# Moving a chunk's word preparation behind the activation's copy on ScalarE, in the first block of an attention, FFN and routed-experts kernel

## The chip, the cores and the metric

The program runs on one core of a Trainium2 chip. Its time is device microseconds (us) of one execution; the kernel before takes 1396.14 us (median of 3 runs, 1395.46 to 1397.46). Five engines work beside each other, each through its own instructions in order: PE (TensorE, matmuls), DVE (VectorE), ACT (ScalarE), POOL (GpSimd) and SP (SyncE, here only an issuer of DMAs). They wait for one another by semaphores.

## The reference, cut to what matters

```python
# 1. attention over 8-fold pooled keys and values, 8 batches x 8 heads, 576 tokens, head size 64
k_p = k.reshape(B, H, 72, 8, D).mean(axis=3); v_p = (the same of v)
attn = softmax(q @ k_p.T / sqrt(D))          # 72 scores a token and head
x = (attn @ v_p) as rows of 512              # 4608 tokens
# 2. a dense FFN, 512 -> 2048 -> 512
h = x @ w_in
g = where(h >= 1, h, where(h <= -1, 0, (h + 1) ** 2 / 4))
x = g @ w_out
# 3. routing to one of 8 experts (512 -> 1024 -> 512, relu), weighted by the gate's probability
out[tokens of e] = gate * (relu(x @ w1[e]) @ w2[e])
```

The dense FFN's weights come in a 64-bit format: `w_in` and `w_out` are read as pairs of 32-bit words, and the kernel makes float32 numbers of them itself.

## The kernel before, in words

The 4608 tokens are 36 tiles of 128 and go through the dense FFN in ten blocks of 3, 4, ..., 4, 3 and 2 tiles. A block runs over 16 chunks `m` of the hidden width. For each chunk, `f1(j, m)` (lines 614 to 643) makes the hidden values of 128 columns for the block's tokens, in one of two PSUM banks (`ps[m % 2]`, the names ps_72 and ps_73), and `f2(j, m)` multiplies them with the chunk's rows of `w_out`. Every product is taken in three matmuls, high by high, high by low and low by high, so each factor is split into a high part (a copy that rounds) and a low part (the difference). `f1` runs two chunks ahead of `f2`.

The activation of a chunk is a relay: DVE clips (L626), ACT squares (L627), DVE takes the larger of that and the hidden value, in the PSUM bank (L631), ACT copies it as the high part (L632), DVE subtracts for the low part (L266 with FG as its output). The next chunk but one overwrites the bank, so its `f1` comes behind that L266. L631 and L632 stand in a function `larger`, L266 in `lower`; both are not issued at once but put on a list `later`, which `flush()` works off. `larger` puts `lower` on the list when it runs, so that comes one flush later.

Between the products of a chunk stand two slots, `slot(j, 2 * m)` behind `f1` and `slot(j, 2 * m + 1)` behind `f2`. A slot runs some units of the attention for the next block's tiles (transpose of the queries L384 and its copy L386; scores L327 with maximum L334 and difference L336; exp L341; sum L394; turning L414 and L416; a way through DRAM, L417 and L423; the product with the values L443 and its copies L449 and L450) and ends with a flush.

In the first block the weights aren't there yet. A `tick` stands at the head of each of the slots 0 to 23. It converts: for the weight chunk at hand, `convert_a` (two ACT instructions, L545 and L549) scales the high words and prepares their sign; `convert_b` puts two DVE instructions (L557 and L560, integer shifts that join the words, through PSUM) on a list `pend`, which `mix()` works off, a call at a time, at certain places of the units and in `f1`, and which the next tick's `mix(4)` empties; two ticks later `convert_c` splits the result (ACT L571, high; POOL L266 with W or WO, low). An even slot's tick splits a chunk of `w_out` (WO), an odd slot's a chunk of `w_in` (W). The next words from DRAM are loaded into the buffer that the tick before has read (L530, L533, on SP).

Because `larger` lies on the list when an even slot begins and the flush stands at the slot's end, ACT's order in an even slot is: square, split (L571), L545, L549, the copies of the units, then L632. The first chunks are converted in a head section, the last ones of it (ticks 4 to 7) between the first two `f1`.

Of the kernel before, what the change touches and what calls it, by code (L numbers as in the profile page):

```python
# [24 lines left out]
def attention_ffn_routed_experts_kernel(  # L25
# [244 lines left out]
    def mix(n=1):  # L270
        for _ in range(min(n, len(pend))):
            pend.popleft()()
# [3 lines left out]
    def flush():  # L276
        for _ in range(len(later)):
            later.popleft()()
# [284 lines left out]
    def convert_ab(i):  # L563
        convert_a(i)
        convert_b(i)

    def convert_c(i):
        m, o = order[i]
        dst, _ = cvt_dst(i)
        hi, lo = (WO[:, m % 4, 0], WO[:, m % 4, 1]) if o else (wi4(m, 0), wi4(m, 1))  # L570
        nc.scalar.activation(out=hi, in_=dst, func=ACTF.Copy)  # L571
        low_part(lo, dst, hi)
        if o:
            nc.sync.dma_start(out=r32(wo_d[m]), in_=r32(WO[:, m % 4]))
# [15 lines left out]
    def more_raw(i):  # L590
        if i < len(order) and order[i]:
            load_raw(*order[i], i % NRB)

    def tick(late=False):

        n = ticks[0]
        mix(4)
        if n > 0:
            more_raw(n - 1 + NRB)
        if 0 <= n - 2 < len(order) and n != 3:  # L600
            convert_c(n - 2)
        if n < len(order):
            if late:
                later.append(lambda: convert_ab(n))
            else:
                convert_ab(n)
        ticks[0] += 1
# [5 lines left out]
    def f1(j, m):  # L613
        g = j * KF + m
        n = blocks[j][1] * 128
        o = ps[m % 2][:, 0:n]
        for c in range(KD):
            xh, xl = XT[:, j % 2, 0, c, 0:n], XT[:, j % 2, 1, c, 0:n]
            nc.tensor.matmul(o, wi(m, 0, c), xh, start=(c == 0), stop=False)  # L619
            nc.tensor.matmul(o, wi(m, 0, c), xl, start=False, stop=False)  # L620
            nc.tensor.matmul(o, wi(m, 1, c), xh, start=False, stop=(c == KD - 1))  # L621
        r = (JK if j == 0 and m % 2 else FR)[:, 0:n]
        gh, gl = FG[:, g % (AHEAD + 1), 0, 0:n], FG[:, g % (AHEAD + 1), 1, 0:n]


        nc.vector.tensor_scalar(r, o, -1.0, 1.0, op0=ALU.max, op1=ALU.min)  # L626
        nc.scalar.activation(out=r, in_=r, func=ACTF.Square, scale=0.5, bias=half)  # L627
        mix()

        def larger():  # L630
            nc.vector.tensor_tensor(out=o, in0=r, in1=o, op=ALU.max)  # L631
            nc.scalar.activation(out=gh, in_=o, func=ACTF.Copy)  # L632
            if KF <= g + 1 < len(steps):
                load_out(g + 1)
            later.append(lower)

        def lower():
            low_part(gl, o, gh, nc.vector)
        later.append(larger)
# [163 lines left out]
    def pick_first():  # L803
        V = nc.vector
        cnt = CB[:, 0]
        mx, mn = MX4[:, 0], MN4[:, 0]
        g = G1[:, 0]
        V.tensor_reduce(out=mx, in_=cnt, axis=AX.X, op=ALU.max)
        V.tensor_scalar(g, cnt, mx, None, op0=ALU.is_equal)
        V.scalar_tensor_tensor(out=g, in0=g, scalar=-16.0, in1=iota4[:, 0], op0=ALU.mult,  # L810
                               op1=ALU.add)
        V.tensor_reduce(out=mn, in_=g, axis=AX.X, op=ALU.min)
        V.tensor_scalar(FST, g, mn, None, op0=ALU.is_equal)
        V.tensor_scalar(FSI, mn, 16.0, None, op0=ALU.add)
        V.tensor_copy(FSR, FSI)

        V.tensor_scalar(POS0, FSI, -float(CAP), -float(EARLY * 128), op0=ALU.mult, op1=ALU.add)
        for t in range(LN):
            V.tensor_scalar(IDF[:, t:t + 1], pcol, float((blocks[-1][0] + t) * 128 - NT), None,
                            op0=ALU.add)  # L820
# [4 lines left out]
    def fetch_first(dst, t0, n):  # L825
        r = nc.values_load(FSR[0:1, 0:1], engines=[SP], min_val=0, max_val=NE - 1)
        nc.sync.dma_start(out=dst, in_=tiles_of[:, bass.ds(r, 1), t0:t0 + n].rearrange(
            "p o r -> p (o r)"))
# [5 lines left out]
    def load_first(i):  # L834
        if not first:
            first.append(nc.values_load(FSR[0:1, 0:1], engines=[ACT], min_val=0, max_val=NE - 1))
        src = (w1, w2)[i // 4][bass.ds(first[0], 1)].rearrange("o (c p) f -> p (o c) f", p=128)

        if i < 4:
            nc.scalar.dma_start(out=ST1[:, i:i + 1], in_=src[:, i:i + 1])  # L840
        else:
            nc.scalar.dma_start(out=ST2[:, 2 * i - 8:2 * i - 6], in_=src[:, 2 * i - 8:2 * i - 6])
# [129 lines left out]
    def q_gather(qn, i):  # L972
        gather(XG[i], q_ids(qn, i), qn == 0)

    def q_tx(qn, i):
        xb, cs = (NB + qn) % 2, slice(i * 128, (i + 1) * 128)
        u_tx(XG[i], XT[:, xb, 0, :, cs], XT[:, xb, 1, :, cs], q_gate(qn, i))
# [104 lines left out]
    def cvt1(c):  # L1082
        nc.scalar.activation(out=e1(0)[:, c], in_=ST1[:, c], func=ACTF.Copy)
        low_part(e1(1)[:, c], ST1[:, c], e1(0)[:, c])

    def cvt2(hf, i):
        cs = slice(4 * hf + 2 * i, 4 * hf + 2 * i + 2)
        nc.scalar.activation(out=e2(0)[:, cs], in_=ST2[:, cs], func=ACTF.Copy)
        nc.vector.tensor_tensor(out=e2(1)[:, cs], in0=ST2[:, cs], in1=r32(e2(0)[:, cs]),
                                op=ALU.subtract)  # L1090
# [41 lines left out]
    with tc.manual_schedule():  # L1132
# [9 lines left out]
        def run_units(n):  # L1142
            for _ in range(n):
                units.popleft()[1]()
            if qloads:
                qloads.popleft()()
# [79 lines left out]
        def slot(j, s):  # L1226

            want = min(state["units"], -(-(s + 1) * state["units"] // (22 if j == NB - 2 else 29 - 2 * AHEAD + 2)))
            wide[0] = False
            if j == 0:  # L1230
                for _ in range(min(1, PER[s // 2]) if s % 2 == 0 else PER[s // 2] - 1):
                    tick()
            run_units(want - state["done"])
            state["done"] = max(want, state["done"])
            flush()
            if j == 0 and kv:
                kv.popleft()()
            for _ in range(2 if j >= NB - 2 else 0 if wide[0] else 1 + s % 2):
                if todo:
                    todo.popleft()()  # L1240
            if j == PICK + 2 and s == 0:
                pick_first()
            for i in range(8):
                if 32 * (j - NB + 2) + s == LF[i]:
                    load_first(i)
            if j == NB - 2:

                if s == 1:
                    fetch_first(IDA, 0, EARLY)
                if s == 9:  # L1250
                    for i in range(EARLY):
                        q_gather(0, i)
            if j == NB - 1:
                if s == 3:
                    nc.gpsimd.iota(IO, pattern=[[1, 128]], base=0, channel_multiplier=0,
                                   allow_small_or_imprecise_dtypes=True)
                if s == 17:
                    fetch_first(IDQ, EARLY, 4 * NQ)
                if s == 27:
                    nc.vector.tensor_copy(IDMF, IDQ)  # L1260
                if s in CV1:
                    cvt1(CV1.index(s))
                if s in QT0:
                    q_tx(0, QT0.index(s))
                if s in (25, 27):
                    cvt2(0, (s - 25) // 2)

        for m in range(AHEAD):
            f1(0, m)
            flush()  # L1270
            while ticks[0] < CAHEAD + 2 + m:
                tick()
                flush()
        for g, (j, m) in enumerate(steps):
            if m == 0:
# [22 lines left out]
            else:  # L1298
                f1e(0, g + AHEAD - len(steps))
            slot(j, 2 * m)  # L1300
            f2(j, m)
            if (j, m) == (0, KF - 2):
# [4 lines left out]
                nc.gpsimd.iota(pr, pattern=[[0, NE * NTILE]], base=NT, channel_multiplier=1)  # L1307
                nc.sync.dma_start(out=perm_t, in_=pr)
            slot(j, 2 * m + 1)
        evict_y(NB - 1)  # L1310
        st, scatters = route_steps(NB - 1, bank)
# [186 lines left out]
```

## Time and profile before

| | |
|---|---|
| median of 3 runs | 1396.14 us |
| the profiled execution | 1394.67 us |
| its span in the trace | 1393.0 us |
| PE busy | 1353.9 us (97%) |
| DVE, ACT, POOL busy | 762.4, 433.3, 355.5 us |

PE's busy share is in tenths 7 7 8 8 in the first four of 40 slices of 34.8 us and 9 in nearly all behind them. The first block's `f1` of chunk 0 starts at 30 us, that of chunk 2 at 36 us and the second block's first `f1` at 138.58 us; this is the stretch that the change touches. Times in the rows are us from the span's start; a duration in a timeline is that of one instruction with its latency, and the next of the same engine can start before it ends.

### The profile page before, as it was taken

What the parts mean: (1) busy time and instruction counts of PE and PEld (TensorE: products, weight loads), DVE (VectorE), ACT (ScalarE), POOL (GpSimd) and SP (SyncE); (2) the same over time, 40 slices, a digit from 0 to 9 for tenths busy, and PEclk for the clock granted to TensorE, in tenths of its full rate; (3) what the DMA queues carried; (4) which work ended last, traced back from release to release, by engine and by line L of the source; (5) the groups of instructions that cost most, each with busy time, mean ns of one, the idle gap of its engine ahead of it and who ended that gap; (6) DMA issues with size and microseconds to landing.
All of it is one profiled execution on the core that took longest, in us unless ns stands there. A gap on an engine that the chain in (4) does not pass through costs nothing. (4 is left out here: it accounts for less than half of the span.)

```text
span 1393.0 us, 22129 instructions
## 1 busy us (share of the span) xinstructions
PE 1353.9 (97%) x8114; PEld 1111.7 (80%) x8114; DVE 762.4 (55%) x1539; ACT 433.3 (31%) x730; POOL 355.5 (26%) x517
## 2 busy tenths in 40 slices
PE   7788999999999999999999999999999999999998
PEld 6666778888778788788788788889878888888886
DVE  5698566656666675566666556455532323323426
ACT  5667232222222222222222233343121111111335
POOL 4475636004304203313310011021231211111211
PEclk9899999999999999999999999999999999999999
DMA  9986656546637555555453344572543223331235
GB/s 235 287 274 221 186 144 193 144 123 176 179 116 197 149 161 155 159 166 150 148 158 111 111 142 146 187 264 79 182 137 107 92 72 109 104 107 59 86 125 188
DMA packets 170702, 213.48 MB, mean 153 GB/s; under 512 B 83431, under 2 KB 114439, under 8 KB 170568
## 3 DMA queue, kind: packets, MB, share of 16 engines
q1 hardware_dynamic: 135992, 102.29, 25.7%
q10 hardware_dynamic: 26784, 88.16, 18.9%
q0 software_dynamic: 7792, 21.35, 4.7%
q8 instruction: 71, 1.16, 0.4%
q14 instruction: 63, 0.52, 0.1%
HBM read 188.30 MB, written 47.03 MB: 169 GB/s over the span
## 5 line engine op out<-in xcount | busy, mean ns | idle before, releaser
L619 PE MATMUL ps<-XT,W 128*128 128x512 f32 (+2 forms) x640 | 243.3, 380 | 5.3 <-ACT W L571 2.4
L621 PE MATMUL ps<-XT,W 128*128 128x512 f32 (+2 forms) x640 | 237.6, 371 | 2.2 <-POOL W L266 2.2
L620 PE MATMUL ps<-XT,W 128*128 128x512 f32 (+2 forms) x640 | 237.6, 371 | 0.5 <-DVE XT L450 0.5
L647 PE MATMUL ps<-WO,FG 128*128 128x512 f32 x576 | 231.2, 401 | 1.0 <-ACT Y L656 1.0
L648 PE MATMUL ps<-WO,FG 128*128 128x512 f32 x576 | 225.9, 392 | 0.0
L649 PE MATMUL ps<-WO,FG 128*128 128x512 f32 x576 | 225.3, 391 | 0.0
L627 ACT ACTIVATE FX<-FX,half 128x512 f32<-128x512 f32 (+2 forms) x152 | 104.0, 684 | 379.7 <-DVE FX L626 357.9
L626 DVE TENSOR_SCALAR FX<-ps 128x512 f32<-128x512 f32 (+2 forms) x152 | 96.9, 638 | 122.0 <-PE ps L621 121.5
L619 PEld LDWEIGHTS ps<-XT,W 128*128 128x128 f32 x640 | 121.3, 190 | 30.4 <-ACT W L571 3.6
L745 POOL DMA_INDIRECT perm_d<-idt,POSI x36 | 35.2, 978 | 424.3 <-DVE SM L731 357.5
L621 PEld LDWEIGHTS ps<-XT,W 128*128 128x128 f32 x640 | 121.3, 190 | 21.4 <-POOL W L266 3.4
L1019 DVE SCALAR_TENSOR_TENSOR FG<-ps,FG 128x512 fp32r<-128x512 f32 (+1 forms) x64 | 43.2, 674 | 173.3 <-ACT FG L1018 173.3
L631 DVE TENSOR_TENSOR ps<-FX,ps 128x512 f32<-128x512 f32 (+2 forms) x152 | 97.6, 642 | 73.5 <-ACT FX L627 73.5
L620 PEld LDWEIGHTS ps<-XT,W 128*128 128x128 f32 x640 | 121.4, 190 | 18.4 <-DVE XT L450 1.1
L647 PEld LDWEIGHTS ps<-WO,FG 128*128 128x128 f32 x576 | 108.4, 188 | 25.7 <-issue 2.8
L632 ACT ACTIVATE FG<-ps 128x512 fp32r<-128x512 f32 (+2 forms) x160 | 88.8, 555 | 125.4 <-DVE ps L631 116.8
L649 PEld LDWEIGHTS ps<-WO,FG 128*128 128x128 f32 x576 | 108.6, 188 | 23.5
L266 DVE TENSOR_TENSOR FG<-ps,FG 128x512 fp32r<-128x512 f32 (+2 forms) x160 | 100.8, 630 | 44.6 <-ACT FG L632 43.1
L648 PEld LDWEIGHTS ps<-WO,FG 128*128 128x128 f32 x576 | 108.6, 188 | 19.8
L1018 ACT ACTIVATE FG<-ps 128x512 fp32r<-128x512 f32 (+1 forms) x64 | 37.4, 584 | 244.1 <-PE ps L1015 230.5
L254 POOL TENSOR_TENSOR AT<-AT 72x256 f32<-72x256 f32 x104 | 79.2, 762 | 128.9 <-DMA AT<-in_v_dram 67.7
L1013 PE MATMUL ps<-XT,W 128*128 128x512 f32 (+1 forms) x256 | 99.0, 387 | 2.9 <-ACT XT L997 2.5
(235 smaller groups left out, 2157.8 us busy)
## 6 DMA issues: line engine op xcount, KB each, us to landing
WO<-wo_d ACTq DMA_DIRECT2D x144, 512.0 KB
AT<-in_moe_w_dram SPq DMA_DIRECT2D x30, 1024.0 KB
p_d<-AT SPq DMA_DIRECT2D x29, 384.0 KB
AT<-in_v_dram SPq DMA_DIRECT2D x59, 144.0 KB
wo_d<-WO SPq DMA_DIRECT2D x16, 512.0 KB
AT<-in_k_dram SPq DMA_DIRECT2D x56, 144.0 KB
PT<-p_d SPq DMA_DIRECT2D x58, 128.0 KB
yrow_d<-Y ACTq DMA_DIRECT2D x7, 1032.0 KB
```

The lines of the kernel that those rows point to most:

```text
L266: eng.tensor_tensor(out=lo, in0=x, in1=r32(hi), op=ALU.subtract)
L619: nc.tensor.matmul(o, wi(m, 0, c), xh, start=(c == 0), stop=False)
L620: nc.tensor.matmul(o, wi(m, 0, c), xl, start=False, stop=False)
L621: nc.tensor.matmul(o, wi(m, 1, c), xh, start=False, stop=(c == KD - 1))
L626: nc.vector.tensor_scalar(r, o, -1.0, 1.0, op0=ALU.max, op1=ALU.min)
L627: nc.scalar.activation(out=r, in_=r, func=ACTF.Square, scale=0.5, bias=half)
L631: nc.vector.tensor_tensor(out=o, in0=r, in1=o, op=ALU.max)
L632: nc.scalar.activation(out=gh, in_=o, func=ACTF.Copy)
L647: nc.tensor.matmul(o, gh, WO[:, g % 4, 0], start=(m == 0), stop=False)
L648: nc.tensor.matmul(o, gh, WO[:, g % 4, 1], start=False, stop=False)
L649: nc.tensor.matmul(o, gl, WO[:, g % 4, 0], start=False, stop=(m == KF - 1))
L1013: nc.tensor.matmul(o, e1(0)[:, c, ms], xh, start=(c == 0), stop=False)
```

## The change

In the first block's slots, and in the short loop that runs ticks 4 to 7, `tick` is called with `late=True`. This does what the head section has done already: `convert_a` and `convert_b` of the tick are put on the list `later` instead of being issued at once. In a slot the list then holds `larger` (or `lower`), `convert_a` with `convert_b`, and what the units add; so L545 and L549 come behind the units' copies and behind L632, and `pend` gets L557 and L560 only at the slot's end. The splits (`convert_c`) and the loads stay where they were. No instruction is added or taken away; PE's, POOL's and SP's orders are the same.

```diff
@@ slot(j, s)
             wide[0] = False
             if j == 0:
                 for _ in range(min(1, PER[s // 2]) if s % 2 == 0 else PER[s // 2] - 1):
-                    tick()
+                    tick(True)
             run_units(want - state["done"])
             state["done"] = max(want, state["done"])
             flush()
@@ before the main loop
             f1(0, m)
             flush()
             while ticks[0] < CAHEAD + 2 + m:
-                tick()
+                tick(True)
                 flush()
```

On ACT, two even slots of the first block, those of chunk 10 and, behind the "...", of chunk 11 (FX and AT hold the clipped values of even and odd chunks, FG the activation, Y, WG and AT also raw words; ps_78 and ps_79 are the units' banks):

```order
 L627 ACTIVATE FX<-FX,half 128x384
 L571 ACTIVATE WO<-FX 128x512
+L632 ACTIVATE FG<-ps_72 128x384
 L545 ACTIVATE FX<-Y 128x512
 L549 ACTIVATE WG<-Y 128x512
-L632 ACTIVATE FG<-ps_72 128x384
 L341 ACTIVATE AT<-AT 128x8x72
...
+L386 ACTIVATE AT<-ps_78 128x512
+L632 ACTIVATE FG<-ps_73 128x384
 L545 ACTIVATE FX<-AT 128x512
 L549 ACTIVATE WG<-AT 128x512
-L386 ACTIVATE AT<-ps_78 128x512
```

L632 has moved ahead of the pair L545, L549, and so has the unit's copy L386; all twelve even slots read so.

On DVE, the slot of chunk 10, where the unit of the scores stands (ps_77 is the bank through which L557 hands its result to L560):

```order
 L336 TENSOR_TENSOR AT<-ps_78,smx_124 128x4x72
 L334 TENSOR_REDUCE smx_124<-ps_79 128x4
+L336 TENSOR_TENSOR AT<-ps_79,smx_124 128x4x72
+L631 TENSOR_TENSOR ps_72<-FX,ps_72 128x384
 L557 SCALAR_TENSOR_TENSOR ps_77<-Y,WG 128x512
-L336 TENSOR_TENSOR AT<-ps_79,smx_124 128x4x72
-L631 TENSOR_TENSOR ps_72<-FX,ps_72 128x384
 L560 SCALAR_TENSOR_TENSOR FX<-FX,ps_77 128x512
 L266 TENSOR_TENSOR FG<-ps_72,FG 128x384
```

L557 has moved from ahead of L631 to behind it; this happens at chunks 7, 10 and 13. At two earlier places an odd slot's L557 moves from ahead of the second L336 to behind L266 and the next L626. In all other steps DVE's order is unchanged, and there L557 stood right behind L631 before too:

```order
L631 TENSOR_TENSOR ps_72<-FX,ps_72 128x384
L557 SCALAR_TENSOR_TENSOR ps_77<-AT,WG 128x512
L560 SCALAR_TENSOR_TENSOR FX<-FX,ps_77 128x512
L266 TENSOR_TENSOR FG<-ps_72,FG 128x384
L626 TENSOR_SCALAR AT<-ps_73 128x384
```

Nothing moved here (the step of chunk 8, the same in both kernels).

## Rows read from the trace of the kernel before

**Rows 1.** Stretches of 20 us: busy us (instructions) by engine, granted clock, DMA.

```profile
100.00:120.00 20.00, 15.78 (x117) 12.85 (x116) 18.75 (x32) 14.39 (x27) 9.21 (x7) 1.00 0.89 304
...
160.00:180.00 20.00, 20.00 (x134) 16.00 (x133) 9.72 (x16) 5.65 (x11) 10.15 (x19) 1.00 0.70 172
```

**Rows 2.** PE's waits, 36 to 160 us: total us, times, longest.

```profile
PE ps L443 <- DMA PT<-p_d: 5.1, 3, 2.5
PE ps L327 <- ACT AT L386: 3.9, 1, 3.9
```

**Rows 3.** Timeline of ACT, chunk 10: start, duration, instruction, [idle before <-releaser].

```profile
111.11 0.49 ACT L632 ACTIVATE FG<-ps 128x384 fp32r<-128x384 f32 x1 [2.79 <-DVE ps L631]
111.50 0.68 ACT L341 ACTIVATE AT<-AT 128x576 f32<-128x576 f32 x1
...
112.59 0.66 ACT L545 ACTIVATE FX<-Y 128x512 f32<-128x512 f32 x1
113.14 0.78 ACT L549 ACTIVATE WG<-Y 128x512 f16<-128x512 f32 x1
113.78 0.60 ACT L627 ACTIVATE AT<-AT,half 128x384 f32<-128x384 f32 x1
```

**Rows 4.** Timeline of DVE, chunks 10 to 13.

```profile
109.50 0.69 DVE L557 SCALAR_TENSOR_TENSOR ps<-Y,WG 128x512 int32<-128x512 int32 x1
110.09 0.45 DVE L336 TENSOR_TENSOR AT<-ps,smx 128x288 f32<-128x288 f32 x1
110.46 0.56 DVE L631 TENSOR_TENSOR ps<-FX,ps 128x384 f32<-128x384 f32 x1
110.92 0.68 DVE L560 SCALAR_TENSOR_TENSOR FX<-FX,ps 128x512 int32<-128x512 int32 x1
...
113.96 0.70 DVE L557 SCALAR_TENSOR_TENSOR ps<-Y,WG 128x512 int32<-128x512 int32 x1 [0.33 <-ACT WG L549]
...
115.37 0.56 DVE L631 TENSOR_TENSOR ps<-AT,ps 128x384 f32<-128x384 f32 x1
116.18 1.27 DVE L557 SCALAR_TENSOR_TENSOR ps<-AT,WG 128x512 int32<-128x512 int32 x1 [0.26 <-ACT WG L549]
...
121.98 0.69 DVE L450 SCALAR_TENSOR_TENSOR XT<-ps,XT 128x512 fp32r<-128x512 f32 x1 [1.48 <-ACT XT L449]
122.59 0.55 DVE L631 TENSOR_TENSOR ps<-FX,ps 128x384 f32<-128x384 f32 x1
123.05 0.69 DVE L557 SCALAR_TENSOR_TENSOR ps<-WG 128x512 int32<-128x512 int32 x1
...
130.93 0.56 DVE L266 TENSOR_TENSOR FG<-ps,FG 128x384 fp32r<-128x384 f32 x1
```

**Rows 5.** Timeline of PE: two matmuls of chunk 9, the first of chunk 15.

```profile
92.86 0.34 PE L620 MATMUL ps<-XT,W 128*128 128x384 f32 x1
...
94.64 0.52 PE L620 MATMUL ps<-XT,W 128*128 128x384 f32 x1
...
132.04 0.44 PE L619 MATMUL ps<-XT,W 128*128 128x384 f32 x1 [0.44 <-ACT W L571]
```

**Rows 6.** Timeline of DVE, the clip of chunk 3.

```profile
55.72 0.56 DVE L626 TENSOR_SCALAR AT<-ps 128x384 f32<-128x384 f32 x1 [4.62 <-PE ps L621]
```

**Rows 7.** DVE's groups, 28 to 145 us: count, busy us, mean ns, idle before.

```profile
L560 DVE SCALAR_TENSOR_TENSOR FX<-FX,ps 128x512 int32<-128x512 int32 x30 | 20.6, 686 | 1.6
L557 DVE SCALAR_TENSOR_TENSOR ps<-WG 128x512 int32<-128x512 int32 x15 | 15.5, 1032 | 1.7 <-ACT WG L549 1.6
L557 DVE SCALAR_TENSOR_TENSOR ps<-Y,WG 128x512 int32<-128x512 int32 x10 | 8.2, 818 | 1.0 <-ACT WG L549 1.0
...
L557 DVE SCALAR_TENSOR_TENSOR ps<-AT,WG 128x512 int32<-128x512 int32 x5 | 4.1, 820 | 2.5 <-ACT WG L549 2.5
```

**Rows 8.** Timeline of DVE, the longest L557.

```profile
98.58 3.17 DVE L557 SCALAR_TENSOR_TENSOR ps<-WG 128x512 int32<-128x512 int32 x1 [0.18 <-ACT WG L549]
```

**Rows 9.** Timeline of POOL beside it.

```profile
99.90 1.29 POOL L266 TENSOR_TENSOR WO<-FX,WO 128x512 fp32r<-128x512 f32 x1
```

## The prediction, before the result was known

> **What bounds the kernel now.** I read the busy shares by stretch first, then PE's waits in the first block, then the timelines of ACT and DVE side by side. Over the whole span PE is the bound. In the first block it is not: from 100 to 120 us PE is busy 15.78 of 20 us and DVE 18.75, while from 160 to 180 us, with the conversion over, PE is busy all of its 20 us and DVE 9.72 [rows 1]. So between about 65 and 135 us the relay of the activation and the conversion, run by DVE and ACT in turns, sets the pace and PE follows. What PE itself names as releaser there is small and mixed: 5.1 us for the transposed probabilities from DRAM, 3.9 us once for ACT's copy of the transposed queries [rows 2]. Whatever is lost or won in this block stays to the end, because behind it PE has no idle time to give back.
>
> **What the change moves.** No instruction comes or goes. In the loop for ticks 4 to 7 the list is flushed right behind the tick, and the order of every engine stays as it was: nothing. In the twelve even slots L545 and L549 go behind the units' copies and L632. Two things follow.
>
> What it gives: L386, L449 and L632 no longer stand behind a pair that takes 1.19 us of ACT (L545 starts at 112.59, the instruction behind L549 at 113.78) [rows 3].
>
> What it takes: L632 cannot start before DVE's L631, so now L545 and L549 cannot either, and DVE's next instruction behind L631 is L557, which needs L549. Before, ACT did this pair while DVE was still on its way to L631. Now DVE stands still while ACT does three instructions. The price from rows: L631 starts at 110.46 and L632 at 111.11, 0.65; L632 to the next ACT instruction 0.39; L545 to L549 0.55; L549 at 113.14 to DVE's L557 at 113.96, 0.82 [rows 3, 4]. From L631's start to L557's start that is 2.41 us, where DVE alone needs 0.46 (122.59 to 123.05) [rows 4]. DVE works in order, so everything behind L557 waits too: L560, L266 (for which PE's next `f1` but one waits, since it overwrites the bank), the clip L626 of the next chunk and the units. No operation here is new, but a wait is; its bounds are 0 (DVE would have stood idle anyway, as the 4.62 us before the clip of chunk 3 [rows 6]) and 1.95 us a chunk. I work with rows of three kinds of steps, which repeat every three chunks:
>
> - Chunk 10 (scores unit; L557 now behind L631): L631 comes 0.59 sooner, at 109.87, L557 at 109.87 + 2.41 = 112.28, L560 after its 0.69 at 112.97 instead of 110.92: 2.05 later.
> - Chunk 11: L557 followed L631 by 0.81 (115.37 to 116.18), now by 2.41; the 0.33 wait at 113.96 falls away, since DVE comes later and finds the signs there: 2.41 - 0.81 - 0.33 = 1.27 later.
> - Chunk 12: 2.41 instead of 0.46, but DVE had waited 1.48 for L449, which comes 1.19 sooner: 2.41 - 0.46 - 1.19 = 0.76 later [rows 4].
>
> Three chunks together: 4.08 us. DVE is busy 94% there [rows 1], so I see nothing that would swallow it.
>
> The sum, chunk by chunk. Chunks 2 and 3: L386 comes 1.19 sooner and PE's 3.9 us wait shrinks, but L557 of that slot is late and stands ahead of the scores' maximum on DVE; DVE then idles for PE (4.62 us [rows 6]). Between -1.2 and +1.9; I take 0. Chunks 4 to 6: DVE begins with idle time in hand, half of a full turn, 2.0. Chunks 7 to 9 and 10 to 12: two full turns, 8.2. Chunk 13: a step like chunk 10's, 2.05, less the slack of PE's `f1` of chunk 15, which starts at 132.04 and could have at 130.93 + 0.56 = 131.49 [rows 4, 5]: 1.5. Behind it no pair is left to move. Together 11.7.
>
> One term is open to both sides: how long L557 takes. Its thirty instances are busy 15.5 + 8.2 + 4.1 = 27.8 us, at L560's mean of 0.686 they would be 20.6: 7.2 us too long [rows 7], the worst 3.17 us, and that one ends 0.56 us after a POOL subtraction of 1.29 us that had begun at 99.90 [rows 8, 9]. L560 has one operand in PSUM, L557 both in SBUF. In the changed kernel the even slots' L557 starts some 2 us later against ACT's split of WO and so against POOL's subtraction behind it; it may miss it, or meet the pooling of the values. Bounds: all 7.2 goes, or all stays. I take half, 3.5, since the even slots hold half of the L557.
>
> The Trainium skill ("SBUF — State Buffer", section "Who interferes with whom") says that a DVE instruction with two SBUF inputs and a GpSimd instruction that reads SBUF exclude each other for a whole instruction, the later one standing still. The trace agrees as far as the rows above go: the long instances are all of L557, up to 3.17 us beside a POOL row. By that rule, if the late L557 missed POOL every time, the sum would be 11.7 - 7.2 = 4.5; by the rows' totals alone, unchanged, 11.7.
>
> Forecast: 11.7 - 3.5 = 8.2 us longer. The profiled execution's 1394.67 becomes 1402.9; the median lies 1.47 above it, so 1404.3 us.
>
> **The rivals.**
>
> 1. The new stall lies in idle time of DVE and only the gain remains. Place: the copies L386 and L449. Price: 1.19 us at the 3.9 us wait for L386 and at each of the three tiles' L449, 4 x 1.19 = 4.8 us shorter, 1391.3 us. It decides if DVE's idle time ahead of the clips is above 1.95 us in most chunks. For it: the 4.62 us at chunk 3 [rows 6]. Against: 1.25 us of idle time in 20 us, over three chunks [rows 1]. Chance 0.08.
>
> 2. A cover: PE waits for the transposed probabilities anyway, 5.1 us [rows 2], and works on in the meantime delayed but not idle; with all of L557's excess gone too, 11.7 - 5.1 - 7.2 = -0.6, 1395.5 us, no change. Against: the transfer starts from DVE's turning of the probabilities, which queues behind the same L557 and moves with it. Chance 0.11.
>
> 3. The clock. PE's matmuls of chunk 9 take 0.52 instead of 0.34 us behind waits of PE [rows 5]: 0.18 x 12 = 2.2 us for an `f1`. Two more such spells on the path: 8.2 + 4.3 = 12.5, 1408.6 us. For it: PE idles more in every chunk. Against: from 100 to 120 us PE idles 4.2 of 20 us and the granted clock is 1.00 [rows 1], and a slower `f1` ends long before DVE comes to its clip. Chance 0.15. The Trainium skill ("TensorE: Matmul & The Clock Gate", section "HAM oscillation — how this bites in real kernels") tells of loops whose repeated waits throw the array back to half rate each time; the row of 0.52 us agrees that it happens here, the stretch at 1.00 that it need not.
>
> That the change does something else than it says is excluded by the order of the instructions.
>
> **How the numbers follow.** Forecast 0.66, rivals 0.08, 0.11 and 0.15. The forecast's own ends are 4.5 (L557's excess gone) and 11.7 (all stays): 1400.6 to 1407.8. The range goes on to the slow clock with none of the excess gone, 11.7 + 4.3 = 16.0 at the worst, of which I take most, and below to 1399, between the forecast's lower end and the cover: 1399.0 to 1411.5. About 0.2% (2.8 us) is what a measurement tells from no change. Slower by more: forecast and clock, 0.81. Within: 0.11. Faster: 0.08.
>
> **What would show it right or wrong.** Right: DVE's idle time ahead of L557, put down to ACT's L549, rises from the 5.1 us of the groups [rows 7] to about 20 us, in pieces of 1.5 to 2 us, one to a chunk from 2 to 13; L632 follows L631 by 0.65 in each; the second block's first `f1` starts some 8 us later than at 138.58, and all behind it is shifted by the same. L557's busy total falls by some 3 us. The wait of 3.9 us for L386 shrinks by about 1.2. Wrong: if the stalls are there but the second block starts within 1 us of before, DVE had slack that I didn't see (rivals 1 and 2); if DVE stalls little, ACT's pair did not become part of the relay; if the shift is over 12 us with the granted clock well under 0.9 between 80 and 140 us, it is the clock.

## The result, and the profile after

The changed kernel takes 1404.45 us (median of 4 runs, 1403.74 to 1406.29) against 1396.57 us of the kernel before (4 runs beside it, 1395.46 to 1397.46). The ratio is 1.0066, 95% interval 1.0053 to 1.0078: slower by 9.2 us, 7.4 to 10.9 (here and below the differences in us are taken from such ratios; the two medians as they stand differ by 7.9). The forecast was 8.2 us longer. The span of the profiled execution grew from 1393.0 to 1403.0 us.

The stretches of 20 us of the changed kernel, in the columns of [rows 1]:

```profile
100.00:120.00 20.00, 15.93 (x123) 12.99 (x124) 14.21 (x27) 13.36 (x24) 7.63 (x6) 0.91 0.80 264
...
160.00:180.00 20.00, 20.00 (x133) 15.98 (x132) 11.59 (x21) 7.17 (x12) 11.29 (x22) 1.00 0.70 175
```

DVE was busy 18.75 us of the first stretch and is now busy 14.21: it stands still, though it sets the pace (the changed kernel is some 5 us behind by then, so the stretches don't hold quite the same work). Behind the block PE is again busy all the time, so nothing is given back.

Where DVE waits in the first block, before (28 to 145 us) and after (28 to 153 us); total us, times, longest:

```profile
DVE XT L450 <- ACT XT L449: 5.2, 5, 1.7
DVE ps L557 <- ACT WG L549: 5.1, 13, 1.1
DVE AT L626 <- PE ps L621: 4.6, 1, 4.6
DVE FX L626 <- PE ps L621: 4.1, 2, 2.7
```

```profile
DVE ps L557 <- ACT WG L549: 23.4, 15, 1.8
DVE AT L626 <- PE ps L621: 5.1, 1, 5.1
DVE XT L450 <- ACT XT L449: 4.2, 5, 1.8
DVE FX L626 <- PE ps L621: 1.7, 2, 1.3
```

One line has grown, by 18.3 us, and its longest is the stall of the forecast. The timelines of ACT and DVE at chunk 10, to be held against [rows 3, 4]:

```profile
115.42 0.49 ACT L632 ACTIVATE FG<-ps 128x384 fp32r<-128x384 f32 x1 [3.43 <-DVE ps L631]
115.80 0.65 ACT L545 ACTIVATE FX<-Y 128x512 f32<-128x512 f32 x1
116.35 0.77 ACT L549 ACTIVATE WG<-Y 128x512 f16<-128x512 f32 x1
```

```profile
114.77 0.55 DVE L631 TENSOR_TENSOR ps<-FX,ps 128x384 f32<-128x384 f32 x1
117.15 0.70 DVE L557 SCALAR_TENSOR_TENSOR ps<-Y,WG 128x512 int32<-128x512 int32 x1 [1.83 <-ACT WG L549]
...
119.86 0.51 DVE L626 TENSOR_SCALAR AT<-ps 128x384 f32<-128x384 f32 x1
...
124.79 0.70 DVE L557 SCALAR_TENSOR_TENSOR ps<-AT,WG 128x512 int32<-128x512 int32 x1 [1.80 <-ACT WG L549]
...
126.60 0.55 DVE L626 TENSOR_SCALAR FX<-ps 128x384 f32<-128x384 f32 x1
...
128.83 0.69 DVE L450 SCALAR_TENSOR_TENSOR XT<-ps,XT 128x512 fp32r<-128x512 f32 x1 [0.29 <-ACT XT L449]
129.44 0.55 DVE L631 TENSOR_TENSOR ps<-FX,ps 128x384 f32<-128x384 f32 x1
131.80 0.70 DVE L557 SCALAR_TENSOR_TENSOR ps<-WG 128x512 int32<-128x512 int32 x1 [1.80 <-ACT WG L549]
```

The relay reads off: L631 at 114.77, L632 at 115.42, L545, L549, L557 at 117.15, 2.38 us from first to last, with ACT idle 3.43 us ahead of it and DVE idle 1.83 us within it. There are twelve such stalls of 1.77 to 1.83 us, one for each chunk from 2 to 13. PE's waits, 36 to 170 us, beside [rows 2]:

```profile
PE ps L619 <- DVE FG L266: 12.1, 7, 2.4
PE ps L384 <- DVE AT L336: 5.2, 4, 2.4
PE ps L443 <- DMA PT<-p_d: 4.7, 3, 1.8
PE ps L327 <- ACT AT L386: 2.8, 1, 2.8
PE ps L327 <- ACT AT L288: 1.8, 1, 1.8
...
```

The wait for L386 is 1.1 us shorter, as the change meant it; the same scores then wait 1.8 us for L288, the copy of the transposed pooled keys, which ACT does behind L632 and so now behind the pair; I had not seen that. What has come is above all the first line: PE waits for the bank that L266 reads, and L266 stands behind L557 on DVE. The second block's first `f1`, at 138.58 us before, now reads (the first of its matmuls)

```profile
149.36 0.40 PE L619 MATMUL ps<-XT,W 128*128 128x512 f32 x1
```

All of DVE's first block lies 0.41 us later from its beginning (the first clip at 32.83 instead of 32.42 us), so the block itself is 10.37 us longer in this trace; below, "shift" is always this measure, with the run's own beginning taken off.

### The profile page after: what moved, and what is told of

The parts are those of the page before. It is cut to its first block, busy times and chain, and to the rows that moved or that the text cites. A ratio compares the mean times of both kernels' runs of the same rounds, so it can differ in the third digit from the quotient of the medians.

```text
span 1403.0 us, 22125 instructions
## 1 busy us (share of the span) xinstructions
PE 1356.3 (97%) x8114; PEld 1114.5 (79%) x8114; DVE 757.9 (54%) x1539; ACT 435.0 (31%) x730; POOL 353.3 (25%) x517
## 5 line engine op out<-in xcount | busy, mean ns | idle before, releaser
L626 DVE TENSOR_SCALAR FX<-ps 128x512 f32<-128x512 f32 (+2 forms) x152 | 96.8, 637 | 120.8 <-PE ps L621 120.2
L631 DVE TENSOR_TENSOR ps<-FX,ps 128x512 f32<-128x512 f32 (+2 forms) x152 | 97.5, 642 | 72.7 <-ACT FX L627 72.7
L632 ACT ACTIVATE FG<-ps 128x512 fp32r<-128x512 f32 (+2 forms) x160 | 88.8, 555 | 129.8 <-DVE ps L631 121.1
L266 DVE TENSOR_TENSOR FG<-ps,FG 128x512 fp32r<-128x512 f32 (+2 forms) x160 | 100.7, 629 | 44.5 <-ACT FG L632 43.1
```

The source lines that it names most:

```text
L266: eng.tensor_tensor(out=lo, in0=x, in1=r32(hi), op=ALU.subtract)
```

## The experiments

**The pair behind the units' copies, but ahead of L632.** All orders but ACT's are the changed kernel's.

```diff
-                later.append(lambda: convert_ab(n))
+                (held if late == 2 else later).append(lambda: convert_ab(n))
...
-                    tick(True)
+                    tick(2)
...
-            state["done"] = max(want, state["done"])
+            state["done"] = max(want, state["done"]); [held.popleft()() for _ in range(len(held))]
             flush()
```

> The pair L545, L549 stands behind the units' copies but ahead of L632; every other order is the changed kernel's, DVE's included. Theory (the pair became part of the relay L631, L632, L545, L549, L557): the idle time of DVE ahead of L557 falls from 23.4 us back to about 5, and the time to that of the kernel before or 1 to 4 us under it (L386 and L449 come 1.19 us sooner): 1392 to 1397 us. Rival (DVE's L557 moved behind L336 and L631, and the units' copies moved ahead, cost the time; or PE's slow clock): DVE's order and the copies are as in the changed kernel, so it stays at 1402 to 1406 us.

Measured: 1395.14 us against 1395.64, ratio 1.0002 (0.9993 to 1.0012); shift -1.1 us. Its DVE waits (28 to 145 us):

```profile
DVE ps L557 <- ACT WG L549: 1.8, 4, 0.9
```

This tells the theory from the rivals: with DVE's order and the units' copies left as changed, putting the pair ahead of L632 alone takes the stall and the whole price away. So neither the moved L557 nor an accident of PE's clock is the cause. It is no better than the kernel before either, which the range of the expectation allowed.

**L266 ahead of the words on DVE.** ACT's order is the changed kernel's; in an odd slot DVE does L266 of the activation first, then L557 and L560 (in the scores' slots of chunks 2 and 4 L557 still comes ahead of L266 and only L560 behind it).

```diff
-        mix(4)
-        if n > 0:
+        mix(0 if hold else 4)
+        if n > 0 and not hold:
             more_raw(n - 1 + NRB)
...
-            state["done"] = max(want, state["done"])
+            state["done"] = max(want, state["done"]); hold and later.insert(1, lambda n=ticks[0]: (mix(4 if len(pend) < 4 else 3), more_raw(n - 2 + NRB)))
             flush()
```

> The changed kernel, with an odd slot's L557 and L560 issued behind L266 of the activation on DVE (and the load that reuses their buffer behind them). L266 frees the bank for PE's next f1 but one. If the stall costs time because PE waits for the bank (12.1 us of waits for L266 in the changed kernel), most of the 8 to 10 us go: 1395 to 1398 us. If it costs time because DVE's own work is stretched, only the 0.47 us of L266 fit into each stall: 12 x 0.47 = 5.6 us less at most, 1399 to 1403 us. Rival (the bank and the stall play no part): 1402 to 1406 us.

Measured: 1400.40 us, ratio 1.0045 (1.0030 to 1.0060), 6.3 us over the kernel before; shift 6.2 us. DVE's and PE's waits:

```profile
DVE ps L557 <- ACT WG L549: 8.9, 14, 1.1
DVE FG L266 <- ACT FG L632: 6.3, 11, 0.6
```

```profile
PE ps L443 <- DMA PT<-p_d: 6.1, 2, 3.9
PE ps L621 <- POOL W L266: 4.0, 6, 0.8
PE ps L619 <- ACT W L571: 3.4, 3, 1.4
```

PE's wait for the bank is gone from the list, and about two thirds of the price are still there. So the bank is where PE shows the loss, and at most a third of it hangs on the bank: DVE's own idle time counts. Ahead of L557 and L266 together it is 15.2 us, 9.0 more than in the kernel before (5.1 + 1.1), for 6.2 us of shift; in the changed kernel 18.3 more for 10.4.

**The pair put off in odd slots alone.**

```diff
-                    tick()
+                    tick(s % 2 == 1)
```

> Only the ticks of odd slots put their pair on the list; even slots as before. ACT's order is that of the kernel before, on DVE two L557 of odd slots move (behind L266 and L626, chunks 3 and 5). Theory: nothing in the relay changes, within 1.5 us of the kernel before. Rival (putting the words off by itself costs): 1400 us or more.

Measured: 1396.09 us, ratio 1.0006 (0.9994 to 1.0018), shift -0.1 us. Putting the words off costs nothing where L632 isn't passed.

**Every other even slot, and the other six.**

```diff
-                    tick()
+                    tick(s % 4 == 0)
```

> Only the ticks of slots 0, 4, 8, ..., 20 put their pair on the list, six of the twelve stalls (chunks 2, 4, 6, 8, 10, 12). Theory: six stalls of 1.8 us on DVE; time about half of the whole change's, 4 to 5 us over the kernel before, somewhat less if the slack between stalls takes part of each: 1398.5 to 1402 us. Rival (one early stall or the slow clock does it): either nothing or nearly the whole 8 to 10 us.

Measured: 1402.61 us, ratio 1.0057 (1.0044 to 1.0070), 8.0 us; shift 6.05 us. That is more than expected from half the stalls, and just above the range; their sizes are 1.77 to 1.83 us as in the whole change. So I ran the other half (`s % 4 == 2`):

> The other six of the twelve even slots (2, 6, 10, 14, 18, 22; chunks 3, 5, 7, 9, 11, 13) put their pair on the list. The first half (chunks 2, 4, ..., 12) shifted the second block by 6.1 us in its trace and the median by about 8; the whole change by 10.4 and 9.2. If each stall costs by itself, this half gives the rest, 4 to 5 us: 1398.5 to 1401.5 us. If a stall costs more where the next step has none, because the two halves compete for the same waiting and for POOL's lock, this half too gives 6 to 8 us alone and the halves sum to more than the whole: 1401.5 to 1404 us.

Measured: 1399.70 us against 1394.72, ratio 1.0029 (1.0017 to 1.0041), 4.0 us; shift 6.3 us. The times sum to 12.0 us against 9.2 for the whole, the shifts to 12.35 against 10.37. (By the medians the halves are 7.0 and 5.0 us longer, 12.0 again.) Timing put this half where single stalls would have it, the trace where the halves compete. The traces agree with each other on more than half for each, but I don't settle how much of the gap between the halves' 8.0 and 4.0 us is the choice of chunks and how much the spread of the runs (1399.14 to 1403.53 and 1397.23 to 1401.24).

**Less of POOL's work beside it.** L557's length was the one term that I could only halve. Sixteen of POOL's additions in the first block are left out, in the kernel before, the changed one, and the one of the first experiment:

```diff
-        eng.tensor_tensor(out=raw[:, 0:256], in0=raw[:, 0:256], in1=raw[:, 256:512], op=ALU.add)
-        eng.tensor_tensor(out=raw[:, 0:128], in0=raw[:, 0:128], in1=raw[:, 128:256], op=ALU.add)
+        if b != 1: eng.tensor_tensor(out=raw[:, 0:256], in0=raw[:, 0:256], in1=raw[:, 256:512], op=ALU.add)
+        if b != 1: eng.tensor_tensor(out=raw[:, 0:128], in0=raw[:, 0:128], in1=raw[:, 128:256], op=ALU.add)
```

> The kernel before, without two of the three additions of the second batch's pooled values on POOL (sixteen instructions in the first block; the pooled values are then sums of two of eight rows, so the routing and the end of the run may differ a little). If L557's long instances come from POOL's instructions beside it, L557's busy total in the first block falls from 27.7 us by 3 us or more and the second block starts 2 to 4 us sooner. If they come from something else, both stay.

> The same part left out of the changed kernel. Theory: the twelve stalls of 1.8 us stay, L557 is short in both, so the change's whole price shows without the relief that L557 gave: the second block starts 10.4 us plus 1 to 4 us later than in the run on the kernel before with the same part left out. If the relief was no part of the sum, the difference stays at 10.4 or less.

> The same part left out of the kernel with the pair behind the units' copies and ahead of L632. That kernel equalled the kernel before while its L557 was busy 30.3 instead of 27.7 us. Theory: what the earlier copies give was eaten by longer L557; with less of POOL's work beside it, the second block starts 1 to 3 us sooner than in the run on the kernel before with the same part left out. If the copies give nothing, within 0.5 us.

Measured, as ratios to the kernel before: 1.0004 (0.9992 to 1.0016), 1.0075 (1.0060 to 1.0091) and 0.9990 (0.9975 to 1.0005); shifts -0.20, 9.58 and -0.49 us. L557's groups, to be held against [rows 7], in the first two:

```profile
L557 DVE SCALAR_TENSOR_TENSOR ps<-WG 128x512 int32<-128x512 int32 x15 | 10.9, 728 | 1.5 <-ACT WG L549 1.4
L557 DVE SCALAR_TENSOR_TENSOR ps<-Y,WG 128x512 int32<-128x512 int32 x10 | 7.1, 707 | 1.0 <-ACT WG L549 1.0
L557 DVE SCALAR_TENSOR_TENSOR ps<-AT,WG 128x512 int32<-128x512 int32 x5 | 4.9, 986 | 2.5 <-ACT WG L549 1.4 <-DMA AT<-in_k_dram 1.1
```

```profile
L557 DVE SCALAR_TENSOR_TENSOR ps<-WG 128x512 int32<-128x512 int32 x15 | 10.4, 694 | 7.8 <-ACT WG L549 7.8
L557 DVE SCALAR_TENSOR_TENSOR ps<-Y,WG 128x512 int32<-128x512 int32 x10 | 8.5, 847 | 7.4 <-ACT WG L549 7.3
L557 DVE SCALAR_TENSOR_TENSOR ps<-AT,WG 128x512 int32<-128x512 int32 x5 | 3.5, 701 | 8.2 <-ACT WG L549 8.2
```

The thirty L557 of the kernel before fall from 27.8 to 22.9 us: its long instances come in good part from POOL's work. But the second block starts only 0.2 us sooner, where 2 to 4 were expected: that expectation failed. The trace shows where the gain went. Counted from clip to clip (L626 to L626), this kernel is 1.8 us quicker than the kernel before in chunks 7 to 9, where the long L557 had stood, and 1.7 us slower in chunks 4 to 6: PE waits 3.0 us for the transposed probabilities, 1.7 in the kernel before, and DVE's clip of chunk 7 waits 3.1 us for PE, where before it waited for nothing.

```profile
75.64 1.97 PE L443 MATMUL ps<-PT,VS 72*64 72x128 f32 x16 [3.02 <-DMA PT<-p_d]
```

```profile
84.30 0.56 DVE L626 TENSOR_SCALAR AT<-ps 128x384 f32<-128x384 f32 x1 [3.08 <-PE ps L621]
```

Between the first and second of these kernels the block grows by 9.58 + 0.20 = 9.8 us, where the expectation had 10.4 plus 1 to 4: it failed too. By chunks it grows by 0.5 us up to chunk 4, 0.4 in chunks 4 to 6, 3.6 in 7 to 9, 3.8 in 10 to 12 and 1.5 behind. So chunks 7 to 9 cost nearly a full turn when L557 is short in both kernels, and chunks 4 to 6 cost little because the first kernel has that new wait at the clip of chunk 7. That the sum stayed at 9.8 doesn't show that L557's length was worth nothing. Each of these is one trace; why the transfer came no sooner was not tried.

The third kernel gains 0.3 us of shift on the first, within the 0.5 of "the copies give nothing". By the times it is some 2 us faster, with intervals that overlap, so a small gain is not excluded.

## Why the prediction was right

**The mechanism** was right in every step that the forecast named: the pair became part of the relay, DVE stands behind it, L626, the units and PE's bank wait behind that, and PE has nothing to give back later. The pair moved back ahead of L632 undoes all of it.

**The price of one turn** was 2.41 us from L631 to L557, measured 2.38; the stall 1.95, measured 1.8. The three kinds of steps, from clip to clip (L626 to L626), after less before: chunk 10, 9.59 - 7.80 = 1.79, forecast 2.05; chunk 11, 6.74 - 5.44 = 1.30, forecast 1.27; chunk 12, 7.93 - 7.22 = 0.71, forecast 0.76 (L450's wait did shrink from 1.48 to 0.29, as the earlier L449 promised); chunk 13, 8.61 - 6.64 = 1.97, forecast 2.05.

**The sum was near in part by luck.** Taken by the clips, the block of the changed kernel is longer by 0.2 us up to chunk 4 (forecast 0), 2.4 in chunks 4 to 6 (forecast 2.0), 2.0 in chunks 7 to 9 (forecast 4.1), 3.8 in chunks 10 to 12 (4.1) and 2.0 from chunk 13 on to the second block's `f1` (1.5): 10.4, where the forecast had 11.7 without the relief from L557 and 8.2 with it. The one turn far off is that of chunks 7 to 9. I had taken the turn of chunks 10 to 12 as a pattern for it, but DVE before had lost time there already: three of its six L557 were far over 0.69 us, the worst of them that of [rows 8], and the six together were busy 8.2 us before and 5.1 after. With less of POOL's work, where the six are busy 5.0 us before the change and 4.9 behind it, the turn costs 3.6. So the 2.1 us that are missing in this turn are, for the most part, the relief from L557 itself, and the forecast's term for it, 3.5 over the whole block, was too large. L557 was shorter by even more, by 4.5 us (11.0 + 8.5 + 3.8 = 23.3 instead of 27.8), but 1.6 of that lay in chunks 4 to 6, which were no quicker for it. The half of 7.2 was the middle between two bounds and had no better ground; with 2.1 in its place the forecast would have been 1405.7 us. The forecast of 8.2 lies within the measured 7.4 to 10.9, but 2.2 us under the block of the trace.

**DVE's account** over the block alone, from the first clip to the second block's `f1` (32.42 to 138.58 us before, 32.83 to 149.36 after), closes: 18.4 us more of waiting for L549, 1.8 less ahead of the clips, 1.8 less ahead of L450, 0.9 less ahead of L334, and 3.6 us less of busy time (85.7 became 82.1) make 10.3, for a block 10.4 us longer. This is bookkeeping on one engine and no second proof.

**The rivals.** That only the gain remains (1391.3) and that a cover hides it (1395.5) are out by the result; the cover's argument, a transfer that PE waits for anyway, is seen failing in PE's waits: 5.1 us for the transposed probabilities before, 4.7 after, so the transfer moved with DVE. The clock: the granted clock did fall from 1.00 to 0.91 in the stretch from 100 to 120 us, and stayed at 0.91 in the two behind it, but it had risen from 0.93 and 0.90 to 1.00 in the two ahead of it, and from chunk 5 to 15 no clip waits for PE, so a slow `f1` ends in time. The clock was not tried by itself, but the kernel with the odd slots alone had a lower one, 0.88, 0.93, 0.93 and 0.93 in the four stretches from 60 to 140 us against the changed kernel's 1.00, 1.00, 0.91 and 0.91, and a shift of -0.1 us. What the clock can have added is some 0.5 us at the end: from the clip of chunk 15 to the second block's `f1` the changed kernel takes 2.8 us, and with less of POOL's work, at 1.00 from 140 to 160 us, 2.25. What the change meant to give, earlier copies, is worth 1.1 us at one wait of PE; the kernel that has it alone took the time of the kernel before.

## What to carry to other kernels

On an engine that works in order, an instruction moved behind another one inherits what that one waits for: moving preparatory work "out of the way" of a result is only free if the work behind it on the other engines doesn't need it before the result's own wait is over. Look for the pair of engines that hand work to and fro, and ask of each moved instruction whether it now stands between two hands of the relay; the price is then the path there and back as far as the waiting engine has nothing else to do in it (here 2.4 us a chunk, of which 1.8 were new waiting), not the instruction's own 1.2 us. And when a term of a sum is "less contention", find out first whether the contended instruction sits where anything waits: 4.9 us less of L557 moved the block by 0.2, because PE's wait for a transfer, and DVE's for PE, took back what the shorter instructions gave.

## What the runs showed of the hardware

DVE's shift L557, both of whose operands lie in SBUF, took 0.69 us or up to 3.17 us; leaving out sixteen of POOL's additions beside it took 4.9 us off its thirty instances, while L560, with one operand in PSUM, stayed at a mean of 686 to 687 ns in all these kernels. The Trainium skill ("SBUF — State Buffer", section "Who interferes with whom") has it that a DVE instruction with two SBUF inputs contends with a GpSimd instruction that reads SBUF, and that one with at most one SBUF input, outside the two-port modes, does not; the two rows agree with it. New to me was how little of such a lock may reach the time: of the 4.9 us, 1.8 showed in chunks 7 to 9, and a later wait took nearly all of that back.
